# Layer 2's weights summed and parked in DRAM during layer 1, its activation moved into the first product, and its second product done with seven products

## The chip, the cores and the metric

One core of a Trainium2 chip runs the whole program. The metric is the device time of one execution in microseconds (us). The profile is one execution taken by the hardware profiler; its span, from the first to the last instruction, is a little shorter than the execution's own time.

## The reference

The program computes windowed attention (4 batches, 8 heads, 576 positions, head size 64, each position sees itself and the 63 before it), then two MLPs over the 2304 tokens of 512 features, each with 2048 hidden features:

```python
scores = np.matmul(q, k.transpose(0, 1, 3, 2)) / np.sqrt(D)
mask = (rel >= 0) & (rel < 64)
attn = softmax(np.where(mask, scores, -1e9))
x = np.matmul(attn, v)                                   # to (2304, 512)

h = x @ w_in;   x = np.maximum(0.01 * h, h) @ w_out      # layer 1, moe_*
h = x @ w_in;   g = np.maximum(h, 0) + np.log1p(np.exp(-np.abs(h)))
out = (g @ w_out).astype(np.float32)                     # layer 2, moe2_*
```

All four weight matrices arrive as 64-bit floats.

## The kernel before, in words

**Numbers.** A 64-bit weight tile (128 x 512) is narrowed to 32 bits by one instruction on ACT and two on DVE (`conv_a`, `conv_b`). Every product is made from two halves of each operand: ACT writes a rounded copy (hi, type fp32r), DVE subtracts it from the value (lo), and `three` issues three matmuls for each product: hi with hi, hi with lo, lo with hi (lines 531 to 533).

**Stages.** A head, written out item by item in the string `HEAD`, loads q, k, v and layer 1's weights, does the first attention blocks and starts layer 1; the order of its items is fixed on every engine. Layer 1 walks six chunks of 384 tokens (`c`); for each of 16 feature blocks `j` it has 12 matmuls of 384 columns (`gemm1`), the activation, the two halves (`gh`, `gl`) and, two steps later (`SKEW`), 12 matmuls into four banks (`gemm2`). The attention of a later chunk is spread over these steps (`attention_slots`); from tile 6 on, q and k are loaded in transposed 32 x 32 blocks straight from the inputs (`load_blocks`). The result of layer 1 goes to DRAM (`x2d`).

Layer 2's **first product** (`products`, lines 604 to 640) uses Winograd's form of Strassen's method: a pair `p` of feature blocks and a chunk `c` of 768 tokens make a 2 x 2 block problem, done with 7 products instead of 8. There are 8 pairs and 3 chunks, 24 steps; a step has 7 products of 6 matmuls with 384 columns each. The sums of tokens (`split_x2`) and of weights (`conv_pair`) are made on DVE by `winograd`, the results are joined by one copy on ACT and seven adds on DVE that read PSUM (line 630), and h goes to DRAM (`hd`). Each pair's weights are loaded, narrowed, summed and split right before their use, by a `ticker` that is called between the steps (`todo`, `prepare`, `later`).

Layer 2's **second product** (`second`) is a plain one: chunks of 512 tokens (`TO`), 16 feature blocks; for a block h is loaded, activated (`activate`: flag the sign on DVE, softplus on ACT, max and add on DVE), split, and multiplied for each of 4 groups of 128 tokens with three matmuls of 512 columns into a bank of its own. Two sets of four banks take turns.

**Queues.** All transfers are issued on the SP queue, in order. PSUM has 8 banks, in the tags `h`, `att` and `o`.

## Time and profile before

| | |
|---|---|
| median of 3 runs | 870.58 us (870.52 to 872.3) |
| the profiled execution | 870.51 us, span 868.7 us |
| TensorE's granted clock | 0.998 of full speed on average |
| PE, busy share of the span | 98%, 5424 matmuls |
| weight loads (PEld) | 92% |
| DVE, ACT, POOL | 62%, 47%, 6% |
| DMA queue, share of 16 engines | 42%, 103.84 MB |

How to read it: PE is the matrix engine, PEld its weight loads, DVE the vector engine, ACT the activation engine, POOL the GpSimd engine and SP the engine whose queue issues the transfers. A group names line, engine and operation, output <- input, shapes and how many; then its busy time, the mean of one, and the idle time before it with what ended that. Records of matmuls overlap, so the interval between two starts says more than a matmul's own duration. In a table by stage the number in brackets is the count of instructions.

### The profile page before, as it was taken

The numbers are of one execution on the slowest core, as the hardware profiler recorded it, in microseconds if no ns is written. First come the engines' busy times: TensorE is split into PE (matmuls) and PEld (weight loads), VectorE is DVE, ScalarE is ACT, GpSimd is POOL, SyncE is SP. The second block draws the span as 40 slices with busy tenths as digits, with TensorE's granted clock in tenths as the row PEclk, the third lists the DMA queues.
The fourth block names the chain that finished last, engine by engine and source line by source line (L and its number), as shares of the span: only waits on it lengthen the run. The fifth ranks groups of instructions, "written<-read, shape, count | busy, mean of one in ns | idle before, by whom it ended". The sixth has DMA issues, their size and how long they took to land.

```text
span 868.7 us, 14599 instructions
## 1 busy us (share of the span) xinstructions
PE 849.8 (98%) x5424; PEld 799.4 (92%) x5424; DVE 537.4 (62%) x1052; ACT 406.2 (47%) x966; POOL 48.7 (6%) x66
## 2 busy tenths in 40 slices
PE   6799999999999999999999999999999999999998
PEld 5689999999999999999999999999999888888886
DVE  5798852535334323323258599777799986766664
ACT  5887742544444334444356433222245654545443
POOL 3211000111111011100000000000000000000000
PEclk9999999999999999999999999999999999999999
DMA  9768552253233421200223245444487553434332
GB/s 206 195 196 244 169 123 36 56 96 89 32 60 75 81 51 49 59 3 13 75 97 102 83 159 191 158 158 158 163 309 260 165 155 102 142 100 142 101 103 66
DMA packets 150278, 104.76 MB, mean 121 GB/s; under 512 B 104896, under 2 KB 129472, under 8 KB 150208
## 3 DMA queue, kind: packets, MB, share of 16 engines
q1 hardware_dynamic: 150208, 103.84, 42.0%
q8 instruction: 42, 0.69, 0.3%
q14 instruction: 28, 0.23, 0.1%
HBM read 75.50 MB, written 28.31 MB: 119 GB/s over the span
## 4 chain that ended last, share of the span: by engine, by line
PE 90%; DVE 3%; DMA 3%; ACT 1%; issue 1%; SPq 1%; POOL 0%; ACTq 0%; DVEq 0%
PE f L533 8%; PE f L532 8%; PE f L531 8%; PE o L531 7%; PE ph L531 7%; PE o L532 7%; PE o L533 7%; PE ph L533 7%; PE ph L532 7%; PE p_s L533 4%; PE p_s L531 4%; PE p_s L532 4%; PE p_a L533 3%; PE p_a L531 3%; PE p_a L532 3%; DMA wraw<-in_moe_w_out_dram 2%
## 5 line engine op out<-in xcount | busy, mean ns | idle before, releaser
L563 DVE TENSOR_TENSOR gl<-g,gh 128x384 fp32r<-128x384 f32 x96 | 57.2, 596 | 174.8 <-ACT gh L557 130.9
L531 PE MATMUL o<-gh,w 128*128 128x384 f32 x384 | 130.9, 341 | 1.9 <-ACT part L577 1.5
L531 PE MATMUL ph<-xh,w 128*128 128x384 f32 x384 | 130.4, 340 | 0.0
L532 PE MATMUL o<-gl,w 128*128 128x384 f32 x384 | 128.7, 335 | 0.7 <-DVE gl L563 0.6
L533 PE MATMUL ph<-xh,w 128*128 128x384 f32 x384 | 128.4, 334 | 0.0
L532 PE MATMUL ph<-xl,w 128*128 128x384 f32 x384 | 128.3, 334 | 0.0
L533 PE MATMUL o<-gh,w 128*128 128x384 f32 x360 | 120.4, 334 | 0.0
L551 ACT ACTIVATE g<-ph 128x384 f32<-128x384 f32 x96 | 46.9, 488 | 144.9 <-PE ph L533 143.6
L531 PE MATMUL f<-w,s 128*128 128x512 f32 x234 | 91.0, 389 | 0.0
L532 PE MATMUL f<-w,s 128*128 128x512 f32 x234 | 91.0, 389 | 0.0
L533 PE MATMUL f<-w,s 128*128 128x512 f32 x234 | 91.0, 389 | 0.0
L662 ACT ACTIVATE s<-s 128x512 f32<-128x512 f32 (+1 forms) x80 | 46.8, 588 | 72.6 <-DVE s L661 72.2
L531 PEld LDWEIGHTS o<-gh,w 128*128 128x128 f32 x384 | 72.1, 188 | 4.4 <-ACT part L577 1.8
L532 PEld LDWEIGHTS o<-gl,w 128*128 128x128 f32 x384 | 72.1, 188 | 1.4 <-DVE gl L563 1.2
L664 DVE SCALAR_TENSOR_TENSOR s<-s,s 128x512 f32<-128x512 f32 (+1 forms) x80 | 50.7, 637 | 36.4 <-ACT s L662 36.0
L531 PEld LDWEIGHTS ph<-xh,w 128*128 128x128 f32 x384 | 72.1, 188 | 1.0 <-issue 0.5
L532 PEld LDWEIGHTS ph<-xl,w 128*128 128x128 f32 x384 | 72.2, 188 | 0.0
L533 PEld LDWEIGHTS ph<-xh,w 128*128 128x128 f32 x384 | 72.1, 188 | 0.0
L533 PEld LDWEIGHTS o<-gh,w 128*128 128x128 f32 x360 | 67.6, 188 | 0.0
L439 ACT ACTIVATE sm<-sm,nm 128x128 f32<-128x128 f32 x144 | 56.0, 391 | 19.6 <-DVE nm L428 19.5
L234 DVE TENSOR_TENSOR s<-s,s 128x512 fp32r<-128x512 f32 (+1 forms) x80 | 50.7, 636 | 12.7 <-ACT s L233 12.5
L233 ACT CAST s<-s 128x512 fp32r<-128x512 f32 (+1 forms) x80 | 46.0, 576 | 23.1 <-PE f L532 20.0
(169 smaller groups left out, 1643.6 us busy)
## 6 DMA issues: line engine op xcount, KB each, us to landing
wraw<-in_moe_w_out_dram SPq DMA_DIRECT2D x32, 512.0 KB, 4.8
wraw<-in_moe_w_in_dram SPq DMA_DIRECT2D x32, 512.0 KB, 4.7
s<-hd SPq DMA_DIRECT2D x64, 256.0 KB, 2.7
hd<-h_xh SPq DMA_DIRECT2D x12, 768.0 KB, 4.5
hd<-h_xl SPq DMA_DIRECT2D x12, 768.0 KB, 4.2
x2d<-x SPq DMA_DIRECT2D x24, 192.0 KB, 1.9
x_stage<-x2d SPq DMA_DIRECT2D x24, 192.0 KB, 2.6
out_dram<-s SPq DMA_DIRECT2D x18, 256.0 KB, 2.4
```

The source lines that it names most:

```text
L233: i = nc.scalar.copy(hi, a)
L234: j = nc.vector.tensor_tensor(lo, a, hi.bitcast(F32), ALU.subtract)
L439: nc.scalar.activation(sm[:, p, :], sm[:, p, :], AF.Exp, bias=nm[:, p : p + 1], accum_out=sums[:, p : p + 1],)
L531: nc.tensor.matmul(ps, wh, xh, start=start, stop=False)
L532: nc.tensor.matmul(ps, wh, xl, start=False, stop=False)
L533: nc.tensor.matmul(ps, wl, xh, start=False, stop=stop)
L551: nc.scalar.activation(g, ph, AF.Prelu, alpha=0.01)
L563: b = nc.vector.tensor_tensor(gl, g, gh.bitcast(F32), ALU.subtract)
L662: nc.scalar.activation(g, g, AF.Softplus)
L664: nc.vector.scalar_tensor_tensor(g, h, 0.0, g, ALU.max, ALU.add)
```

## The change

- Layer 2's weights are handled in layer 1's chunks 2 to 5, 32 units in all (`stash`): load, narrow, add the four sums on POOL, write to DRAM (`wd`). For `w_out` they are summed over the other index. The last six units (pairs 5 to 7 of `w_out`) are also split there. Later a pair is loaded ready-summed (`load_row`) and split (`split_pair`): the low half on DVE for `w_in`, on POOL for `w_out`; pairs 5 to 7 need no split.
- q and k from tile 6 on are first laid out in DRAM (`lay_out`, DRAM to DRAM in 128-byte pieces, partly during the head) and loaded from there in one transfer each.
- The sums of x for the first product move from DVE to POOL, and the four that are split get a place of their own (`split_sums`).
- The activation follows each step of the first product: sign flag on DVE, softplus and relu on ACT, add on POOL, and the activated value goes to `hd`.
- The second product uses seven products as well. A step is a pair of feature blocks and 512 tokens (256 in the last chunk): four sums (`sums`) and three low halves on DVE, three hi copies on ACT (`spread`), then per product 3 matmuls of 256 columns for each 256 tokens. Seven banks collect a chunk; at its end `put_out` joins them by the same copy and seven adds. The order on every engine is fixed from the second product on (`ordered`).

```diff
@@ -64,6 +64,7 @@
     CUT = 8
     TB = 32
     BY_DVE = 6
+    THIRDS = 10
     AHEAD = 4
...
     hd = [dp.tile([P, 2, NT], F32, name=f"hd{p}") for p in range(NF // 2)]
+    HD = DM // 2
+    PARTS = 2 * NP * (P // TB)
+    qd, kd = (dp.tile([P, NP, NT], F32, name=f"{nm}d") for nm in "qk")
+    SPLIT, SPAN = 5, 88
+    split_too = lambda i, p: i == 1 and p >= SPLIT
+    wd = [
+        [dp.tile([P, 8, 2, 2, P] if split_too(i, p) else [P, 8, 2, P], F32, name=f"wd{i}_{p}") for p in range(NF // 2)]
+        for i in range(2)
+    ]
 
...
+    ODD = (("v", 3, 1), ("kT", 2, 1), ("qbd", 1, 2), ("part", 1, 3))
+    EVEN = (("raw", 2, 1),) * 2 + (("v", 3, 1),) * 2 + (("sm", 3, 1),) * 2 + (("kT", 2, 1),)
+    ENDS = (("xh", 2, 3), ("xl", 2, 3), ("w_last", 1, 1))
...
+    def load_row(i, p, row, o):
+        if split_too(i, p):
+            nc.sync.dma_start(row.bitcast(F32), wd[i][p][:, o].rearrange("p a h x -> p a (h x)"))
+        else:
+            nc.sync.dma_start(row[:, 1].bitcast(F32), wd[i][p][:, o].rearrange("p h x -> p (h x)"))
...
+        for t in pair_tiles.pop((i, p)):
+            split(t[:, :, 0], t[:, :, 1], t[:, :, 1].bitcast(F32), nc.gpsimd if i == 1 else None)
+
...
+    def stash_load(u):
+        i, p, q = units[u]
+        j = slice(2 * p * P, 2 * (p + 1) * P)
+        if i == 0:
+            src = moe2_w_in[:, j].rearrange("(h q p) f -> p q h f", p=P, q=2)[:, q]
+        else:
+            src = moe2_w_out[j, q * HD : (q + 1) * HD].rearrange("(f p) x -> p f x", p=P)
+        nc.sync.dma_start(raw_of(u).rearrange("p (n x) -> p n x", n=2), src)
+
...
+        def sums_of(u):
+            t = blocks(a_of(u))
+            b = [[t[:, n], t[:, m]] for n, m in ((0, 2), (1, 3))]
+            if units[u][0] == 1:
+                b = [list(x) for x in zip(*b)]
+            winograd([t[:, 4 + n] for n in range(4)], b, units[u][0] == 0, nc.gpsimd)
...
+        at, end = {}, 0
+        light = sum(not has_low(u) for u in range(len(units)))
+        for u in range(len(units)):
+            parts = [(0, stash_load, u + 1), (0, narrow_a, a_of, u), (1, narrow_b, a_of, u), (2, sums_of, u)]
+            if has_low(u):
+                parts += [(2, high, u, 0), (3, low, u, 0), (3, high, u, 1), (4, low, u, 1)]
+            parts += [(7 if has_low(u) else 5, put, u)]
+            for n, *do in parts:
+                at.setdefault(end + n, []).append(do)
+            end = (u + 1) * SPAN // light if u + 1 <= light else end + 4
+        stash_load(0)
+        for n in range(max(at) + 1):
+            yield
+            for f, *x in at.get(n, ()):
+                if x[0] is a_of:
+                    f(a_of(x[1])[:, :DM], raw_of(x[1]))
+                elif f is not stash_load or x[0] < len(units):
+                    f(*x)
+        kept["end"] = True
 
     def key(g):
         return g if isinstance(g, int) else "%d_%d" % g
...
+    def lay_out(b, parts):
+
+
+        for n in parts:
+            src, dst = ((q, qd), (k, kd))[n % 2]
+            p, i = divmod(n // 2, P // TB)
+            h, d = divmod(i * TB, D)
+            s0 = max(BY_DVE * P - b * S, 0)
+            nc.sync.dma_start(
+                dst[i * TB : (i + 1) * TB, p, b * S + s0 : (b + 1) * S].rearrange("r (n c) -> r n c", c=TB),
+                src[b, 2 * p + h, s0:, d : d + TB].rearrange("(n r) c -> r n c", r=TB),
+            )
...
                 for n in range(7)
             ]
-        winograd([ts[:, n] for n in range(4)], b, False)
-        for d, a in zip(XB[c], (b[0][0], b[1][0], b[1][1], *(ts[:, n] for n in range(4)))):
+        winograd([ts[:, n] for n in range(4)], b, False, nc.gpsimd)
+        for d, a in zip(XB[c], (b[0][0], b[1][0], b[1][1])):
             split(d[:, 0, kk], d[:, 1, kk], a)
+
+    def split_sums(c, kk):
+        for n, d in enumerate(XB[c][3:]):
+            split(d[:, 0, kk], d[:, 1, kk], stage["t"][:, n])
 
 
     G = {}
...
+    ORDER = ((0, 0), (5, 4), (6, 5), (4, 3), (2, 1), (7, 2), (3, 6))
...
+        behind.append(
+            combine(
+                (product(*o) for o in ORDER), t("q1"), t("u2"), t("u3"), t("v"),
+                ((h[:, 0, :TH], h[:, 0, TH:]), (h[:, 1, :TH], h[:, 1, TH:])),
+            )
+        )
+        for a in range(2):
+            g = next(act_places)
+            nc.vector.tensor_scalar(g.bitcast(I32), h[:, a].bitcast(I32), -(2**31), None, ALU.bitwise_or)
+            nc.scalar.activation(g, g, AF.Softplus)
+            nc.scalar.activation(h[:, a], h[:, a], AF.Relu)
+            nc.gpsimd.tensor_tensor(g, h[:, a], g, ALU.add)
+            nc.sync.dma_start(hd[p][:, a, c * 2 * TH : (c + 1) * 2 * TH], g)
+
...
+    def sums(i):
+        m = steps2[i][2] // 2
+        h = HT["in"][i % HS][:, :2, : 2 * m]
+        st = kept["64"][1 + i % 2].bitcast(F32)
+        ts = st[:, : 4 * m].rearrange("p (n x) -> p n x", n=4)
+        ready[i] = h, ts
+        winograd([ts[:, x] for x in range(4)], [[h[:, c, r * m : (r + 1) * m] for c in range(2)] for r in range(2)], True)
+
+    def places_of(i):
+        w0, w1, *one = sets[i % SETS]
+        m = steps2[i][2] // 2
+        one = [w[:, :m] for w in one]
+        two = [w[:, 2, : 2 * m].rearrange("p (a x) -> p a x", a=2) for w in (w0, w1)]
+        four = [w[:, :2].rearrange("p a x -> p (a x)")[:, : 4 * m].rearrange("p (n x) -> p n x", n=4) for w in (w0, w1)]
+        return one, two, four, m
+
+    def spread(i):
+        one, two, four, m = places_of(i)
+        h, ts = ready.pop(i)
+        parts = (two, h[:, :, :m]), (one, h[:, 1, m:]), (four, ts)
+        first = [nc.scalar.copy(hi, a) for (hi, lo), a in parts][0].ins
+        last = [nc.vector.tensor_tensor(lo, a, hi.bitcast(F32), ALU.subtract) for (hi, lo), a in parts][-1].ins
+        behind.append((first, last))
+        A[i] = {0: [t[:, 0] for t in two], 2: [t[:, 1] for t in two], 3: one}
+        for x in range(4):
+            A[i][4 + x] = [t[:, x] for t in four]
+
+    def advance(i):
+
+        for f, n in ((sums, 3), (spread, 2), (load_h, 5)):
+            if (HS if f is load_h else 0) <= i + n < len(steps2):
+                f(i + n)
+
+    R = {}
+
...
+    def second(i):
...
+            if first:
+                R[k][x] = next_bank([P, 2, HD], f"f_{k}_{x}")
+            wh, wl = w[USED[ob]]
+            before = None
+            for u in range(nu):
+                cs = slice(u * P, (u + 1) * P)
+                gh, gl = (t[:, cs] for t in a[oa])
+                ps = R[k][x][:, u]
+                j = nc.tensor.matmul(ps, gh, wh, start=first and u == 0, stop=False, skip_group_check=True)
+                if before is not None:
+                    tc.add_manual_dep(
+                        j.ins, before.name,
+                        mybir.DependencyInfo(mybir.DependencyClass.NoSync, mybir.DependencyReason.DATA),
+                        reason="bank",
+                    )
+                nc.tensor.matmul(ps, gh, wl, start=False, stop=False, skip_group_check=True)
+                j = nc.tensor.matmul(ps, gl, wh, start=False, stop=end, skip_group_check=True)
+                before = j.ins
+            return R[k][x][:, :nu]
+
+        made = [product(x) for x in range(7)]
+        if end:
+            split_out = lambda t: t.rearrange("p u (q x) -> p u q x", q=2)
+            ends[i] = [split_out(t) for t in made], [split_out(t[:, :nu]) for t in stage["t4"]]
+
+    ends = {}
...
+    def put_out(i):
+        if i in ends:
+            k, t0, n, p = steps2[i]
+            made, temps = ends.pop(i)
+            res = [r[:, : n // (2 * P)] for r in stage["res"]]
+            halves = [r.rearrange("p u (q c x) -> p u q c x", q=2, c=2) for r in res]
+            combine(iter(made), *temps, [[r[:, :, :, c] for c in range(2)] for r in halves])
+            for r in range(2):
+                r0 = t0 + r * (n // 2)
+                nc.sync.dma_start(out[r0 : r0 + n // 2, :].rearrange("(u p) d -> p u d", p=P), res[r])
+
+    def last_places():
...
+    relay = {f"G{CUT + NF - AHEAD - 2 + n}": (lay_out, first, range(n * PARTS // 2, (n + 1) * PARTS // 2)) for n in range(2)}
+    relay |= {f"G{CUT + NF - AHEAD + n}": (lay_out, first + 1, range(n * PARTS // 4, (n + 1) * PARTS // 4)) for n in range(4)}
...
             slot += 1
             if u == 0:
...
+                later(next, keeper, None, lag=1)
+        if c == 0 and j >= NF - 4:
+            lay_out(3, range(4 * (j + 4 - NF), 4 * (j + 5 - NF)))
+        if c == 2 and 4 <= j < 12:
...
-
+    todo[1] += [(split_x, 2, 0), (split_sums, 2, 0), (load_x, 2, 1)]
+    todo[2] += [(split_x, 2, 1), (split_sums, 2, 1)]
+    for p in range(2, NPR):
+        n = last_of[p - 2] if p < NPR - 1 else 8
+        todo[n] += [(load_first, p)]
+        todo[n + 2] += [(split_pair, 0, p)]
...
+    def load_second(p):
+        if p == 0:
+            tiles = tiles_of((("at", 2, 1),) * 2, "wp1_0") + early(5)
+        elif p == 1:
+            tiles = early(7)
+        else:
+            tiles = tiles_of((ODD, ENDS, EVEN)[p - 2], f"wp1_{p}")
+        load_pair(1, p, tiles)
+
+    def temporaries():
+        stage["t4"] = [w[:, 2].rearrange("p (u x) -> p u x", u=2) for w in HT["in"]]
...
+    todo[N - 3] += [(load_second, 2), (split_pair, 1, 1)]
+    todo[N - 2] += [(advance, -1), (load_second, 3)]
+    todo[N - 1] += [(last_places,), (split_pair, 1, 2), (load_second, 4)]
     for n, (p, c) in enumerate(order):
         products(n, p, c)
...
+        next(rows)
+    late = [rows for rows in late for n in range(7)]
+    temporaries()
     for i in range(len(steps2)):
-        second(*steps2[i], active.pop(i))
-        activate_next(i + 3)
-        load_next(i + 6)
-        if i % 2:
-            later(next, last, None)
+        ordered(queues, second, i)
+        ordered(queues, advance, i)
+        if i < 2:
+            ordered(queues, split_pair, 1, 3 + i)
+        for n in range(4):
+            if late:
+                ordered(queues, next, late.pop(0))
+        ordered(queues, put_out, i)
 
 
 # ---- launch: one core; inputs and outputs as the reference has them ----
```

Where the order shows it. On PE, the start of the second product (`f` is a bank; before, the moving operand is a row of `w_out`, afterwards a row of a pair's weights `wp`, `wq`). Before:

```order
L531 MATMUL f_0_7347<-w2xh,s_7067 128x512
L532 MATMUL f_0_7347<-w2xl,s_7067 128x512
L533 MATMUL f_0_7347<-w2xh,s_7068 128x512
L531 MATMUL f_1_7348<-w2xh,s_7067 128x512
L532 MATMUL f_1_7348<-w2xl,s_7067 128x512
L533 MATMUL f_1_7348<-w2xh,s_7068 128x512
```

Now:

```order
L792 MATMUL f_0_7676<-wp_0_at_7129,a_0_7125 128x256
L799 MATMUL f_0_7676<-wp_0_at_7129,a_0_7125 128x256
L800 MATMUL f_0_7676<-wp_0_at_7129,a_1_7126 128x256
L792 MATMUL f_0_7676<-wp_0_at_7129,a_0_7125 128x256
L799 MATMUL f_0_7676<-wp_0_at_7129,a_0_7125 128x256
L800 MATMUL f_0_7676<-wp_0_at_7129,a_1_7126 128x256
L792 MATMUL f_1_7683<-wq_5_7131,a_0_7125 128x256
```

A bank now takes two groups of three, each of half the columns, with a weight load before every matmul as before.

On ACT, in the first product around the copies of the first bank of steps 8 and 9 (`q`; `h_xh` and `h_xl` take turns as h). Before:

```order
L632 COPY q_8_6115<-p_a_6119 128x384
L159 ACTIVATE cvp_10_6327<-wraw_10_0_6323 128x512
L233 CAST wp_v_6248<-cvp_9_6110 128x256
L233 CAST wp_raw_6246<-cvp_8_6109 128x512
L233 CAST wp_v_6249<-tt_6241 128x512
L159 ACTIVATE cvp_11_6328<-wraw_11_0_6325 128x512
L632 COPY q_9_6179<-p_a_6183 128x384
```

Now:

```order
L699 ACTIVATE kept_2_1589<-kept_2_1589 128x768
L700 ACTIVATE h_xl<-h_xl 128x768
L699 ACTIVATE cv<-cv 128x768
L700 ACTIVATE h_xl<-h_xl 128x768
L707 COPY q_8_6318<-p_0_6322 128x384
L236 CAST wp_4_raw_6389<-wp_4_raw_6389 128x256
L236 CAST wp_4_sm_6393<-wp_4_sm_6393 128x256
```

The four activations of step 7 (line 699 is softplus, 700 relu) stand between the splits before them and the copy of step 8's first bank.

On DVE, in the second product at the end of the first chunk (`in` is h as loaded or a temporary, `kept` the sums, `a` the halves, `res` the output). Now:

```order
L760 TENSOR_TENSOR a_1_7126<-in_7120,a_0_7125 128x512
L760 TENSOR_TENSOR a_gl<-in_7120,a_gh 128x256
L760 TENSOR_TENSOR a_1_7126<-kept_2_1589,a_0_7125 128x1024
L706 TENSOR_TENSOR in_7120<-f_1_7683,in_7119 128x512
L706 TENSOR_TENSOR in_7121<-f_2_7690,in_7120 128x512
L706 TENSOR_TENSOR in_7365<-f_3_7697,in_7120 128x512
L706 TENSOR_TENSOR res_xl<-f_3_7697,in_7121 128x4x128
L706 TENSOR_TENSOR res_xh<-f_4_7704,in_7119 128x4x128
L706 TENSOR_TENSOR res_xh<-f_5_7711,in_7365 128x4x128
L706 TENSOR_TENSOR res_xl<-f_6_7718,in_7121 128x4x128
L255 TENSOR_TENSOR kept_2_1589<-in_7365 128x256 x2
```

The seven adds that empty a chunk's banks come after the low halves for two steps ahead and before the next sums; before, a chunk was emptied by four copies on ACT and four on DVE between the activations.

## Rows read from the trace of the kernel before

**Rows 1.** Busy time by stage; columns: stretch, us, busy us and instructions by engine, clock, DMA.

```profile
0.00:91.40 91.40, 76.77 (x612) 69.96 (x612) 72.68 (x142) 70.08 (x198) 17.87 (x32) 0.98 0.80 208
91.40:493.80 402.40, 402.16 (x2940) 392.65 (x2941) 173.17 (x340) 183.72 (x486) 30.88 (x34) 1.00 0.28 68
493.80:668.60 174.80, 174.80 (x1010) 174.80 (x1009) 149.82 (x298) 53.35 (x100) 0.00 (x0) 1.00 0.57 195
668.60:864.70 196.10, 196.10 (x866) 162.04 (x864) 141.14 (x272) 98.69 (x183) 0.00 (x0) 1.00 0.41 121
```

**Rows 2.** What PE waited for, 91.4 to 868 us: total, times, longest in us.

```profile
PE o L531 <- ACT part L577: 1.5, 1, 1.5
PE ps L703 <- ACT at L467: 0.2, 1, 0.2
```

**Rows 3.** Timeline of PE, first product: start us, us, instruction.

```profile
499.83 0.33 PE L532 MATMUL p_s<-xb,wp_sm 128*128 128x384 f32 x1
...
501.91 0.33 PE L532 MATMUL p_a<-xb,wp_raw 128*128 128x384 f32 x1
```

**Rows 4.** Timeline of PE, second product.

```profile
759.82 0.39 PE L531 MATMUL f<-w2xh,s 128*128 128x512 f32 x1
...
761.86 0.39 PE L531 MATMUL f<-w2xh,s 128*128 128x512 f32 x1
```

**Rows 5.** Instruction groups, second product: count, busy us, mean ns, idle before.

```profile
L531 PE MATMUL f<-w,s 128*128 128x512 f32 x234 | 91.0, 389 | 0.0
L531 PE MATMUL f<-w2xh,s 128*128 128x512 f32 x54 | 21.0, 389 | 0.0
```

**Rows 6.** 128-column matmuls of the head, and weight loads.

```profile
12.97 1.17 PE L413 MATMUL ps<-kT,qbd 128*128 128x128 f32 x9
...
L413 PE MATMUL ps<-kT,qbd 128*128 128x128 f32 x96 | 13.3, 294 | 0.0
L413 PEld LDWEIGHTS ps<-kT,qbd 128*128 128x128 f32 x96 | 12.8, 212 | 0.1
L531 PEld LDWEIGHTS f<-w,s 128*128 128x128 f32 x234 | 43.9, 188 | 9.1
```

**Rows 7.** Instruction groups on DVE.

```profile
L234 DVE TENSOR_TENSOR s<-s,s 128x512 fp32r<-128x512 f32 x64 | 43.9, 689 | 7.5 <-ACT s L233 7.5
L661 DVE TENSOR_SCALAR s<-s 128x512 int32<-128x512 int32 x64 | 26.9, 425 | 1.6 <-DMA s<-hd 0.2
L630 DVE TENSOR_TENSOR v<-p_s,u 128x384 f32<-128x384 f32 x24 | 13.4, 559 | 5.5 <-PE p_s L533 5.4
L234 DVE TENSOR_TENSOR wp_qbd<-cvp,wp_qbd 128x256 fp32r<-128x256 f32 x4 | 1.7, 420 | 0.0
```

**Rows 8.** Instruction groups on ACT and POOL.

```profile
L662 ACT ACTIVATE s<-s 128x512 f32<-128x512 f32 x64 | 40.1, 631 | 66.0 <-DVE s L661 65.7
L632 ACT COPY q<-p_a 128x384 f32<-128x384 f32 x24 | 11.4, 474 | 65.5 <-PE p_a L533 59.7 <-DVE xb L234 5.9
L452 POOL TENSOR_TENSOR sm<-sm,sums 128x512 f32<-128x512 f32 x36 | 38.7, 1075 | 147.3 <-DVE sums L448 103.1 <-PE o L532 23.3 <-ACT w L221 11.3
```

**Rows 9.** Instruction groups of a weight's conversion.

```profile
L159 ACT ACTIVATE cvp<-wraw 128x512 f32<-128x512 f32 x28 | 18.7, 674 | 13.0 <-DMA wraw<-in_moe_w_out_dram 9.2 <-DVE h_xl L630 3.7 <-DMA wraw<-in_moe_w_in_dram 0.2
L176 DVE SCALAR_TENSOR_TENSOR cvp<-wraw,cvp 128x512 uint16<-128x512 uint32 x32 | 23.7, 751 | 0.2
```

**Rows 10.** Timeline of the end, PE and DVE.

```profile
864.32 0.39 PE L533 MATMUL f<-w,s 128*128 128x512 f32 x1
...
865.14 0.42 DVE L680 COPY s<-f 128x256 f32<-128x256 f32 x1 [0.26 <-ACT s L679]
```

**Rows 11.** Timelines of DVE and POOL in layer 1.

```profile
255.41 1.09 DVE L563 TENSOR_TENSOR gl<-g,gh 128x384 fp32r<-128x384 f32 x1 [0.54 <-ACT gh L557]
...
255.04 1.04 POOL L452 TENSOR_TENSOR sm<-sm,sums 128x512 f32<-128x512 f32 x1 [0.52 <-DVE sums L448]
...
306.77 0.56 DVE L563 TENSOR_TENSOR gl<-g,gh 128x384 fp32r<-128x384 f32 x1
```

412 lines of the change are left out of this document (200 added, 212 removed).

## The prediction

> **What bounds the kernel now.** The first view to read is the table of busy time by stage [rows 1]. The span falls into a head up to 91.4 us, layer 1 up to 493.8, layer 2's first product up to 668.6 and its second product up to 864.7. The granted clock is 0.98 in the head and 1.00 afterwards, the upper of TensorE's two levels, 2.4 GHz. After the head PE is busy for 402.16 of 402.40 us, then for all of 174.80 and all of 196.10. Busy time alone proves little, since the records of matmuls overlap; so the second view is what PE waited for [rows 2]: 1.7 us in two places in layer 1, nothing in layer 2. Third, the starts: in the first product 12 intervals of a 384-column matmul lie between 499.83 and 501.91 us, 173.3 ns each [rows 3]; in the second, 9 intervals of a 512-column matmul between 759.82 and 761.86, 226.7 ns each [rows 4]. The first product has 24 steps of 42 matmuls: 1008 x 173.3 ns = 174.7 us. The second has three lines of 234 + 54 matmuls [rows 5]: 864 x 226.7 ns = 195.9 us. Both are the stage's length within 0.2 us. So layer 2 is a string of matmul starts without a hole. It gets shorter only through fewer columns, and longer only when something that feeds PE comes too late. DVE is the busiest feeder: 149.82 of 174.80 us in the first product. POOL does nothing in layer 2 [rows 1].
>
> **Second product by seven.** The new loop has 7 products per pair of feature blocks, for each 3 matmuls per unit of 256 tokens: 42 in a step of 512 tokens, 21 in the last chunk's. Four chunks of 8 pairs and one short one give 32 x 42 + 8 x 21 = 1512 matmuls of 256 columns, in place of 864 of 512: an eighth fewer columns. No row shows this kind of matmul with 256 columns. The line through the two nearest rows falls by 53.4 ns per 128 columns (226.7 - 173.3), so 256 columns would follow every 119.9 ns, and the stage would take 1512 x 0.120 = 181.4 us. From above it is bounded by the 384-column matmul, 173.3 ns: 262.0 us. From below by 128-column matmuls of the head: nine in 1.17 us, of which the last takes some 0.294, so (1.17 - 0.294) / 8 = 110 ns [rows 6]: 166.3 us. What could lift it off the line is the weight load that goes with every matmul, since it has to be over within one interval. Loads of the second product last 188 ns in the records, those of the head's 128-column matmuls 212 ns, and those pass every 110 ns all the same [rows 6]; so a load should fit under 120 ns. I take the line: 195.9 - 181.4 = **14.5 us less**. Break-even is 195.9 / 1512 = 129.6 ns.
>
> The Trainium skill's page TensorE: Matmul & The Clock Gate, Back-to-back issue gap, gives columns / 2.4 + 2.5 ns, which is 109 ns for 256 columns and would make the stage 165 us. For 512 columns it gives 216 ns where the row shows 226.7, so here the rows decide.
>
> **What feeds the second product.** A full step lasts 42 x 0.120 = 5.04 us on PE. On DVE it has four sums of 256 columns at 0.42 us [rows 7] and three low halves of 512, 256 and 1024 columns at 0.69, 0.42 and (an estimate: the first two rows' slope carried on) 1.23 us: 4.0 us. At the end of a chunk seven adds out of PSUM come on top, 512 columns wide; at 0.56 for 384 [rows 7] that is 0.69 each by the same slope, 4.9 us. Eight steps: 37 of 40.3 us. These adds stand in DVE's queue behind the halves for two steps ahead, which PE needs only 5 us later, and a chunk's eighth bank lets the next one begin before they are through. Cost nothing; if DVE were 10% dearer it would set the pace.
>
> **Activation inside the first product.** A step is 42 x 173.3 = 7.28 us. It keeps ACT's copy and DVE's seven adds (7 x 0.56 = 3.9), and gets two flag instructions on DVE over 768 columns (at most 1.5 x 0.425 = 0.64 each [rows 7]), four activations on ACT (at most 1.5 x 0.631 = 0.95 [rows 8]) and two adds on POOL (at most 1.5 x 1.075 = 1.6 [rows 8]). With about 0.8 us of weight splits DVE comes to 6.0, ACT to some 5, POOL to 3.2: each fits. The wait that it adds: a step's activations stand in ACT's queue ahead of the next step's copy of its first bank. That copy, 0.47 us [rows 8], ends at most 0.56 + 0.64 + 4 x 0.95 + 0.47 = 5.5 us after the step's end; PE wants the bank eight products later, 8.3 us after it. Covered with 2.8 us to spare, so nothing. The 150 us of DVE lose the weight conversions and the sums of x, which is the room for it.
>
> **Weights summed in layer 1.** 32 units, each one ACT instruction of 0.67 us and two on DVE of at most 0.75 [rows 9], four POOL sums; the last six also split. ACT gets 22 us more and DVE at most 48, in 402.40 us where they are busy for 183.72 and 173.17 [rows 1]. PE uses a step's halves two steps (8 us) later, so a queue that is a few us late costs nothing. Traffic: 16.8 MB read, some 20 MB written, 6.3 MB more for the relay of q and k, 43 MB or 107 GB/s on top of 68 [rows 1]; the first product moves 195 GB/s without a wait of PE. The SP queue carries writes that wait for POOL ahead of loads of q, k and v; the next tile's loads have some 20 us. Nothing; 0 to +5 at the bounds.
>
> **Head and tail.** Eleven relay transfers are issued between the last weight loads of layer 1, when PE has work in hand: 0 to +1. At the end the last matmul starts at 864.32, the last copy at 865.14, and the output lands at 868.7 [rows 10]. Afterwards adds of 256 columns (about 0.42) trail a product of 0.36 us, and DVE is an instruction further behind: +0.5.
>
> **Sum.** The profiled execution took 870.51 us, 1.8 more than its span, and 0.07 less than the median of 870.58. 870.51 - 14.5 + 0.5 = **856.5 us**.
>
> **Rivals.** *The weight load shows.* On top of 384 / 2.4 = 160 ns of columns the row has 13 ns more [rows 3]. If that stretch followed not the columns but a load of 110 ns, the interval would be 123 to 126 ns, the stage 186 to 190.5 us, the time 861 to 866. For it: load and columns are about equally long here for the first time. Against it: the head's short matmuls have no such stretch.
>
> *A shorter interval*, the 110 ns of the 128-column rows: 166.3 us, time 841. Against it speaks the fixed 13 ns in both stages of layer 2. The Trainium skill's 109 ns (TensorE: Matmul & The Clock Gate, Back-to-back issue gap) would lead to the same place.
>
> *Slower: DVE blocked by POOL in the first product.* In layer 1 a DVE instruction with both operands in SBUF began at 255.41, while a POOL multiply ran from 255.04 to 256.08; it took 1.09 us, where the same line took 0.56 at 306.77, and ended 0.4 after POOL's [rows 11]. POOL, now idle there, would work 3.2 us of each step, plus the sums of x and the splits of five pairs near the hand-over. If three quarters of a step's 3.2 us fall on flags and splits, DVE needs 6.0 + 2.4 = 8.4 us against 7.28, and 24 steps cost 27 us: 883. It decides once the blocked time passes 1.3 us a step and eats the gain at 1.9. Against it: POOL starts when ACT is through, so while DVE does adds out of PSUM, and no row shows those blocked. The Trainium skill's page SBUF — State Buffer, Who interferes with whom, calls this an exclusive lock held for the whole instruction, and its rule spares adds that read PSUM. The trace agrees for the blocked instruction.
>
> *The eighth goes, but the time doesn't.* The weights of pairs 5 to 7 get their places only when the first product ends, and the writes of its last steps share the queue; or layer 1 stalls on a queue. A dozen us lost gives 866 to 871.
>
> **Chances.** The forecast 0.65 (its own range 854 to 861), the load 0.13, the shorter interval 0.04, DVE blocked 0.11, the gain lost 0.07. A measurement tells about 0.2% from no change. The first three are faster: 0.82; the lost gain is the same: 0.07; the blocked DVE slower: 0.11. The range 853 to 871 leaves out the shorter interval and the slower case, 0.15, and a little of the rest.
>
> **What would show it.** Starts of 256-column matmuls 120 ns apart, the second product's stage near 181 us, the first still 174.7 with no wait of PE in the list, layer 1 over at 494. Flags of 0.6 us on DVE; 1.5 or more there, and PE waiting for adds, would mean the block. 125 ns between starts would mean the load. It is wrong if PE waits over 5 us in layer 2, or if the first product's stage grows.

## The result and the profile after

The changed kernel takes 883.59 us (median of 4 runs, 879.79 to 886.33), the kernel before, beside it, 870.55 us (869.98 to 872.3). The ratio is 1.0143, with a 95% interval of 1.0096 to 1.019: 1.4% slower, clear of no change, outside the range, and close to the 883 that the prediction had given to its slower rival. The profiled execution took 881.52 us with a span of 879.7, against 870.51 and 868.7 before. (In the text VectorE is DVE of the rows, ScalarE is ACT, and a place is a stretch of SBUF, the core's on-chip memory, that the program uses in turns.)

The first view is again the table by stage, now of the changed kernel (stretch, length, busy us and instructions of PE, PEld, DVE, ACT and POOL, granted clock, DMA share, GB/s). It answers to [rows 1].

```profile
0.00:91.40 91.40, 79.09 (x626) 72.59 (x627) 75.00 (x147) 72.22 (x201) 18.18 (x32) 0.98 0.83 211
91.40:492.70 401.30, 399.81 (x2928) 389.75 (x2928) 212.08 (x382) 203.65 (x525) 110.39 (x178) 1.00 0.65 172
492.70:691.00 198.30, 182.88 (x1011) 178.09 (x1009) 171.26 (x276) 107.05 (x178) 108.35 (x63) 0.97 0.48 160
691.00:875.40 184.40, 182.09 (x1512) 181.65 (x1512) 155.86 (x298) 79.26 (x134) 20.48 (x14) 1.00 0.47 151
```

Layer 1 ends 1.2 us earlier than before (the first product starts at 492.72 instead of 493.94), although it now holds the stash of weights. The first product, which took 174.80 us, takes 198.30; the second, which took 196.10, takes 184.40. In starts of matmuls: -1.2 before the first product, +22.5 in it (197.0 us from its first start to its last, 174.5 before), +1.1 between the two, -11.3 in the second (184.4 against 195.7), nothing at the tail. That is +11.1 us, and the spans differ by 11.0.

The second view is the list of PE's waits after the head, which held 1.7 us before [rows 2].

```profile
PE p L593 <- DVE u L706: 7.6, 7, 2.5
PE p L593 <- DVE h_xl L706: 3.9, 1, 3.9
PE f L792 <- DVE h_xl L706: 2.3, 1, 2.3
PE p L593 <- ACT q L707: 1.7, 2, 1.1
PE p L593 <- DVE h_xh L706: 1.3, 1, 1.3
```

The banks of the first product (p) come free too late, because VectorE's adds out of them are late. Third, the starts of the second product's matmuls, which answer to [rows 4]: nine intervals lie between these two rows.

```profile
759.75 0.28 PE L800 MATMUL f<-wq,a 128*128 128x256 f32 x1
...
760.83 0.28 PE L800 MATMUL f<-wq,a 128*128 128x256 f32 x1
```

That is 120.0 ns for 256 columns, the value that the line through the two older rows gave. So the eighth was gained, and lost again, twice over, in the stage before. Why VectorE is late there is seen in two timelines of the same four microseconds, VectorE first and then POOL (start us, us, instruction; "x2" joins two in a row).

```profile
509.25 1.74 DVE L237 TENSOR_TENSOR xb<-x_stage,xb 128x384 fp32r<-128x384 f32 x1
510.91 0.55 DVE L706 TENSOR_TENSOR h_xl<-p,u 128x384 f32<-128x384 f32 x1
511.38 1.74 DVE L698 TENSOR_SCALAR kept<-h_xl 128x768 int32<-128x768 int32 x1
```

```profile
508.40 4.30 POOL L701 TENSOR_TENSOR cv<-h_xh,cv 128x768 f32<-128x768 f32 x2
```

While POOL does its two adds (508.40 to 512.70), a low half of 384 columns takes VectorE 1.74 us, where it took 0.55 before, and ends 0.42 us after the first of the two adds (508.40 to 510.57). The flag takes 1.74, where 0.55 is its time with POOL at rest, and ends 0.42 us after the second. The add that reads a PSUM bank stands between them and takes its usual 0.55. A hole of PE follows where several such instructions meet in a row (VectorE, POOL, then PE):

```profile
568.21 2.61 DVE L237 TENSOR_TENSOR wp_xh<-wp_xh 128x768 fp32r<-128x768 f32 x1
570.74 2.56 DVE L237 TENSOR_TENSOR wp_xl<-wp_xl 128x768 fp32r<-128x768 f32 x1
573.23 0.55 DVE L706 TENSOR_TENSOR u<-p,q 128x384 f32<-128x384 f32 x1
```

```profile
568.04 1.96 POOL L701 TENSOR_TENSOR cv<-h_xh,cv 128x768 f32<-128x768 f32 x1 [3.49 <-ACT h_xh L700]
569.96 2.53 POOL L701 TENSOR_TENSOR kept<-h_xh,kept 128x768 f32<-128x768 f32 x1
```

```profile
570.96 0.34 PE L595 MATMUL p<-xb,wp_part 128*128 128x384 f32 x1
573.83 0.44 PE L593 MATMUL p<-xb,wp_part 128*128 128x384 f32 x1 [2.53 <-DVE u L706]
```

POOL is held in turn: its second add takes 2.53 us, where 1.92 is the mean of its kind, and VectorE's `wp_xh` runs into it until 570.82.

For each run below two numbers are taken from its trace. **Lost time** is what VectorE's instructions of the first product took beyond the time of the same form with POOL at rest (0.41 us for 256 columns, 0.55 for 384, 0.68 for 512, 0.95 for 768, 1.22 for 1024, 0.55 for a flag), counted where it is over 0.15 us. **Holes** are the time from the start of that stage's first matmul to the end of its last, less 1008 x 173.3 ns. The changed kernel has 40.1 us lost in 35 instructions and 22.6 us of holes. All 161 adds out of PSUM in its records took 0.55 us, 84 of them with POOL at work. Of VectorE's instructions that leave PSUM alone, 38 began while POOL was computing. 35 of these lost time, and they are all that did; each ended within its own usual time after the end of the POOL instruction beside which it had begun.

### The profile page after: what moved, and what is told of

The parts are those of the page before. It is cut to its first block, busy times and chain, and to the rows that moved or that the text cites. A ratio compares the mean times of both kernels' runs of the same rounds, so it can differ in the third digit from the quotient of the medians.

```text
span 879.7 us, 16530 instructions
## 1 busy us (share of the span) xinstructions
PE 844.1 (96%) x6072; PEld 822.1 (93%) x6072; DVE 615.3 (70%) x1104; ACT 462.2 (53%) x1037; POOL 257.4 (29%) x287
## 5 line engine op out<-in xcount | busy, mean ns | idle before, releaser
L625 DVE TENSOR_TENSOR gl<-g,gh 128x384 fp32r<-128x384 f32 x96 | 59.9, 624 | 130.6 <-ACT gh L619 108.0
L792 PE MATMUL f<-wq,a 128*128 128x256 f32 x252 | 71.4, 283 | 0.0
L799 PE MATMUL f<-wq,a 128*128 128x256 f32 x252 | 71.3, 283 | 0.0
L800 PE MATMUL f<-wq,a 128*128 128x256 f32 x252 | 71.3, 283 | 0.0
L510 POOL TENSOR_TENSOR sm<-sm,sums 128x512 f32<-128x512 f32 x36 | 38.6, 1072 | 87.7 <-DVE sums L506 54.3
L759 ACT CAST a<-in 128x512 fp32r<-128x512 f32 (+1 forms) x40 | 23.0, 576 | 56.7 <-issue 46.8
L760 DVE TENSOR_TENSOR a<-kept,a 128x1024 fp32r<-128x1024 f32 (+1 forms) x40 | 47.9, 1197 | 6.7 <-ACT a L759 6.7
L619 ACT CAST gh<-g 128x384 fp32r<-128x384 f32 x96 | 49.3, 514 | 2.4
```

The lines of the kernel that those rows point to most:

```text
L510: nc.gpsimd.tensor_tensor(sm, sm, sums.unsqueeze(2).to_broadcast([P, NP, P]), ALU.mult)
L619: a = nc.scalar.copy(gh, g)
L625: b = nc.vector.tensor_tensor(gl, g, gh.bitcast(F32), ALU.subtract)
L760: last = [nc.vector.tensor_tensor(lo, a, hi.bitcast(F32), ALU.subtract) for (hi, lo), a in parts][-1].ins
L792: j = nc.tensor.matmul(ps, gh, wh, start=first and u == 0, stop=False, skip_group_check=True)
L799: nc.tensor.matmul(ps, gh, wl, start=False, stop=False, skip_group_check=True)
```

## The experiments

Three theories stood. *Lock*: VectorE's instructions whose operands all lie in SBUF stand still while POOL works there. *ScalarE's queue*: softplus and relu stand ahead of the next step's bank copy. *SP's queue*, added later: the store waits for POOL's add, and loads of weights stand behind it. The edits are in `products` unless said otherwise. The kernel before, measured beside each group of runs, had medians of 870.6 to 872.3 us, so 1 to 2 us between runs of different groups say little.

### Without POOL's add

```diff
-            nc.gpsimd.tensor_tensor(g, h[:, a], g, ALU.add)
```

> Edit: in the first product POOL's add of the relu and the softplus is left out (the softplus alone is stored, so this part of the activation is not computed); flags, softplus, relu, transfers and every order stay. Lock theory (VectorE's instructions whose operands all lie in SBUF stand still while POOL runs: 40.9 us of VectorE time lost in the first product, and TensorE's 23.5 us of holes come from there): POOL falls from 108 to about 25 us in that stage, the lost VectorE time to under 12 us, the holes to under 6 us, the time to 862 to 867 us. Queue theory (ScalarE's softplus and relu stand ahead of the next step's bank copy, and VectorE waits 20.3 us for that copy): nothing in that queue changes, the holes stay at 18 us or more, the time at 878 us or more.

856.73 us, ratio 0.9834 (0.9804 to 0.9865). Lost time 9.6 us, holes 0.2. Its two stages of layer 2:

```profile
493.40:668.10 174.70, 174.70 (x1010) 174.70 (x1009) 144.01 (x279) 107.88 (x180) 23.73 (x19) 1.00 0.54 183
668.10:849.60 181.50, 181.50 (x1513) 181.36 (x1511) 151.29 (x296) 78.44 (x133) 12.07 (x10) 1.00 0.46 152
```

PE is busy throughout both again, 174.7 and 181.5 us long. The split that took 2.61 us takes 0.95:

```profile
L237 DVE TENSOR_TENSOR wp_xh<-wp_xh 128x768 fp32r<-128x768 f32 x1 | 0.9, 950 | 0.0
```

So the whole loss comes through this one instruction per half step; the forecast for everything else in the change holds.

### Without the relu

```diff
-            nc.scalar.activation(h[:, a], h[:, a], AF.Relu)
```

> Edit: in the first product ScalarE's two relu per step are left out (POOL adds the softplus to the plain value, so this part of the activation is not computed); POOL's add stays. Queue theory: the chain copy, seven adds, flag, softplus and relu is 7.15 us long where no wait lengthens it, against 7.28 us of TensorE per step; without the relu it is about 5.7, VectorE's 20.3 us of waits for the copy fall under 5 and the time to 860 to 867 us. Lock theory: POOL still runs 108 us in that stage and VectorE still loses about 40 us; with 171 us of work in 174.7 us most of the holes stay: 872 us or more.

887.72 us, ratio 1.0187 (1.0165 to 1.021). VectorE's waits for the copy fall from 20.3 to 1.5 us, as the queue theory said, and the holes stay: 24.4 us, with 40.4 lost. The order on ScalarE does not make the loss by itself. But the edit changes something else too: VectorE now waits for casts of weights instead (11.2 us for those of one group of tiles), while SP stands 130 us at stores that wait for POOL.

### Softplus and relu a step later

The flags stay; the rest is collected in a list and issued after the next step's copy.

```diff
+        with tc.issue_after(behind[-1][0]):
+            activate(stage.pop("due", ()))
+        if n < len(order) - 3:
+            stage["due"] = due
...
```

> Edit: nothing is left out; softplus and relu of a step are issued behind the next step's bank copy, in all steps but the last three, which stay as in the changed kernel. VectorE's waits for the copy fall from 20 to under 3 us, its standstills beside POOL stay near 40 us. Standstills alone: between the changed kernel's 883.6 and 876; with both needed for the loss it would be 866 us or less.

875.1 us, ratio 1.0043 (1.0026 to 1.006); lost 44.4, holes 13.8. In the last seven steps only three places take turns, and a late activation reads a place that a newer flag has overwritten: that part of the activation is changed there. A first form, late in every step, gave 876.78 us with 41.8 lost and 10.6 of holes; 860 to 867 us had been expected of it if the queue makes the loss, 872 or more if the lock does. The standstills are as long as ever, but fewer of them reach PE: the order decides how many.

### POOL's other work on VectorE

```diff
-        winograd([ts[:, n] for n in range(4)], b, False, nc.gpsimd)
+        winograd([ts[:, n] for n in range(4)], b, False)
...
-            split(t[:, :, 0], t[:, :, 1], t[:, :, 1].bitcast(F32), nc.gpsimd if i == 1 else None)
+            split(t[:, :, 0], t[:, :, 1], t[:, :, 1].bitcast(F32))
```

> Edit: nothing is left out; POOL's other work of the first product and the start of the second (block sums of the input, low halves of layer 2's second weights, 24.5 us on POOL in that stage) goes to VectorE, the activation's add stays on POOL. Lock theory: VectorE takes about 11 us of work more and loses about 9 us less to POOL: within 5 us of the changed kernel's 883.6. Queue theory: the same, no change. If the late holes (after 640 us, where POOL's low halves lie and the clock falls to half) come from those low halves, the time falls by 5 to 8 us.

877.12 us, ratio 1.0064 (1.0042 to 1.0086); lost 28.2, holes 16.7. Less on POOL helps even where VectorE has to do it. Both theories had expected no more than 5 us; the 6.5 that came lie in the 5 to 8 which the expectation gave to the low halves late in the stage.

### The add aside

```diff
-            nc.gpsimd.tensor_tensor(g, h[:, a], g, ALU.add)
+            nc.gpsimd.tensor_tensor(h[:, a], h[:, a], h[:, a], ALU.add)
```

> Edit: POOL's add stays in place and length, but adds the relu to itself in its own place, and nothing waits for it but the next use of that place; the softplus alone is stored (this part of the activation is not computed). It parts POOL's presence from POOL's place in the chain to the store. If VectorE's standstills beside POOL make the loss: the first product loses what the changed kernel loses, 878 to 888 us. If the loss came because stores, places and loads waited for POOL's result: 857 to 864 us, as without the add.

868.03 us, ratio 0.9952 (0.9937 to 0.9968): neither of the two. Lost 29.6, holes 9.6. The instruction is not the twin that it was meant to be: with one place instead of two it takes 1.57 us in place of 1.92. So POOL's presence alone costs some 11 us against the run without it. How much of the other 15 us is the shorter instruction and how much the store that no longer waits for POOL, this run by itself does not tell; but SP still stood 101 us at those stores, now waiting for ScalarE, against 123 us in the changed kernel.

### The add by an accumulating transfer

```diff
-            nc.gpsimd.tensor_tensor(g, h[:, a], g, ALU.add)
+            nc.gpsimd.dma_start(out=g, in_=h[:, a], accum_op=ALU.add)
```

> Edit: nothing is left out; the add of relu and softplus is made by an accumulating transfer from POOL's queue, SBUF to SBUF, ahead of the store, instead of by POOL itself. If POOL's own instruction on SBUF is what stops VectorE, the loss goes as without the add: 857 to 864 us, VectorE's lost time under 16 us. If the extra 0.39 MB per half step, or the work of POOL in issuing it, gets in the way (transfers already take 48% of the queues in that stage), 865 us or more, with waits for places.

903.0 us, ratio 1.0354 (1.0326 to 1.0382). The lost time is gone, 8.8 us, and the holes are 38.5. SP's stores now wait for the accumulating transfers, and its loads of weights wait behind them (what SP waited for, from 493 to 705 us):

```profile
SPq L702 <- DMA kept<-h_xh: 44.6, 10, 13.1
SPq L702 <- DMA cv<-h_xh: 27.6, 9, 9.8
SPq L702 <- DMA kept<-h_xl: 22.7, 8, 5.3
SPq L702 <- DMA cv<-h_xl: 17.0, 5, 6.4
```

ScalarE stands 17.7 us at the casts of one group of weights, 55.5 us at all of them, with the bank copy behind it. This is mostly SP's queue at work, without the lock; VectorE also waited some 20 us for places.

The same add made in DRAM, behind the store of the relu:

> Edit: nothing is left out; the relu is stored first and the softplus is then added onto it in DRAM by an accumulating transfer from POOL's queue. Same reasoning: 857 to 864 us if only POOL's instruction on SBUF costs; two transfers in a row must land before the loads of the second product, so the last step of the first product may make the second product wait some us.

902.65 us, ratio 1.0356 (1.0324 to 1.0387); lost 8.8, holes 33.4. Here the transfers from POOL took 7.4 us to land, and the flags waited 28 us for their places.

### The store from POOL's queue

```diff
-            nc.sync.dma_start(hd[p][:, a, c * 2 * TH : (c + 1) * 2 * TH], g)
+            nc.gpsimd.dma_start(hd[p][:, a, c * 2 * TH : (c + 1) * 2 * TH], g)
```

> Edit: nothing is left out; the store behind POOL's add is issued from POOL's queue instead of SP's, so that SP, whose next orders are the loads of weights, no longer stands at that store until POOL is done. Third theory (SP's queue: the store holds up weight loads, ScalarE stands at the casts of those weights, and the bank copy behind them is late): 865 to 872 us. Standstills of VectorE alone: they stay at 40 us, and the time stays above 878 us.

897.53 us, ratio 1.0299 (1.0269 to 1.0329): worse than the changed kernel. SP no longer stands at the store, ScalarE waits only 2.0 us for weights, and the holes are 37.0 all the same: they don't need SP's queue. Lost time rises to 51.7 us. VectorE's longest wait in the stage is not one for POOL's work, though the profile names POOL there. VectorE, then POOL, then the time from that store's issue to its landing:

```profile
645.50 0.42 DVE L255 TENSOR_TENSOR kept<-in 128x256 f32<-128x256 f32 x1 [3.94 <-POOL cv L701]
```

```profile
640.06 0.56 POOL L702 DMA_DIRECT2D hd<-kept  x1
DMA to landing us min/median/max: 5.4/5.4/5.4
```

The block sum writes the place `kept`, from which that store was still going out. It lands at 645.42, and the sum begins at 645.50. An issue alone did not stop VectorE either: 25 of its instructions on SBUF met nothing of POOL's but an issue, and none took over 0.02 us longer. What raised the lost time is in part this: 8 of the 32 instructions that lost time began ahead of POOL's add, in the issue before it, and 5 stood through more than one POOL instruction. Neither happened in the changed kernel. Why an issue between POOL's adds does that is open.

### The add at loading

Softplus and relu are both stored, the relu in `hr`, a second array like `hd`; in `load_h` an accumulating load adds them.

```diff
+            nc.sync.dma_start(hr[p][:, a, c * 2 * TH : (c + 1) * 2 * TH], h[:, a])
...
+            nc.gpsimd.dma_start(out=HT["in"][i % HS][:, :2, :n], in_=hr[p][:, :, t0 : t0 + n], accum_op=ALU.add)
```

> Edit: nothing is left out; POOL's add is gone from the first product, softplus and relu are both stored, and the second product's load of the softplus is followed by an accumulating load of the relu from POOL's queue (POOL has nothing else there). If POOL's instruction on SBUF beside VectorE is the cause, the first product runs without holes as in the run without the add: 856 to 862 us in all. If the accumulating loads come late, the second product waits for its block sums: 865 us or more.

951.39 us, ratio 1.0919 (1.089 to 1.0948). The first product runs nearly without holes (4.8 us, 8.6 lost), as the lock theory has it; the second takes 272.7 us. Its waits, on VectorE and on POOL:

```profile
DVE kept L256 <- DMA in<-hr: 114.6, 31, 15.5
```

```profile
POOL in L739 <- issue: 118.9, 23, 9.1
POOL in L739 <- DMA in<-hd: 50.7, 6, 14.9
```

POOL is late in issuing, for most of the time without anything that the profile names. VectorE is not what holds it: it worked on SBUF in 44.1 of those 118.9 us. The landing times show what does. All 23 issues came 0.3 us after the accumulating load before had landed, so these loads went one at a time, 6.1 us each in the median. Why they did is open; in the two runs with accumulating transfers in the first product these overlapped. By the Trainium skill's page SBUF — State Buffer, Who interferes with whom, a transfer issued by POOL can starve beside VectorE. This trace does not show that.

### Half of each add

```diff
-            nc.gpsimd.tensor_tensor(g, h[:, a], g, ALU.add)
+            nc.gpsimd.tensor_tensor(g[:, :TH], h[:, a, :TH], g[:, :TH], ALU.add)
```

> Edit: POOL adds only the first half of each place's columns (the other half of the activation lacks its relu). Dose: POOL runs some 45 us less in that stage. Standstill theory: VectorE's lost time falls from 40 to about 22 us and the loss of 27 us (883.6 against 856.7 without the add) to a half or less: 862 to 870 us. If it is POOL's being in the chain at all, not its length, 876 us or more.

858.89 us, ratio 0.9859 (0.9831 to 0.9887); lost 14.0, holes 0.2. A half of the dose leaves not a half of the loss but nearly nothing: the loss is not proportional to POOL's work. Two things help here, and this run doesn't part them: VectorE has 30.7 us of idle time in the run without the add (174.70 less 144.01) that can take some lost time, and half an add is also a shorter instruction.

### Late, and stored from POOL's queue

Softplus and relu a step later, in the first sixteen steps, and the store from POOL's queue, together.

> Edit: nothing is left out; softplus and relu are issued behind the next step's bank copy in the first sixteen steps, and the store goes from POOL's queue. Both together take away VectorE's waits for the copy and SP's stand at the store, and leave POOL's 108 us as they are. If these orders only make a given standstill dear: 863 to 870 us with VectorE's lost time still near 40 us. If the standstills alone set the loss: 872 us or more.

894.18 us, ratio 1.0275 (1.0246 to 1.0303); lost 66.0, holes 35.8. Stores from POOL's queue cost more than the order gives.

### The same work in shorter instructions

```diff
-            nc.gpsimd.tensor_tensor(g, h[:, a], g, ALU.add)
+            for b in range(2):
+                s = slice(b * 2 * TH // 2, (b + 1) * 2 * TH // 2)
+                nc.gpsimd.tensor_tensor(g[:, s], h[:, a, s], g[:, s], ALU.add)
```

Two pieces:

> Edit: nothing is left out; each add of 768 columns on POOL is two of 384 in a row, so POOL's whole time grows a little (about 2 x 1.0 us in place of 1.92) and each instruction is half as long. If VectorE stands only until the POOL instruction in hand ends and then has its turn: lost time 40 to about 25 us or less, 862 to 873 us. If it stands until POOL has no more work: lost time 40 us or more, 880 us or more.

Four pieces:

> Edit: nothing is left out; each add on POOL is four of 192 columns. If VectorE has its turn between instructions: lost time under 20 us, 858 to 868 us; POOL's own time grows by its fixed part and may become late instead. If VectorE stands until POOL has no more work: 880 us or more.

Two give 873.63 us, ratio 1.0031 (1.0017 to 1.0045), with 26.7 us lost and 11.4 of holes; four give 871.1, ratio 1.0005 (0.9988 to 1.0022), with 19.4 lost and 7.6 of holes. From the changed kernel to two and to four pieces POOL works longer, 109.8, 125.4 and 145.6 us in the stage, and VectorE loses less. Two pieces lost 1.7 us more than the 25 expected, and the times are 0.6 and 3 us above their ranges. In these runs the second product waits too: from first start to last it takes 187.0 and 189.0 us, 181.3 without the add. One group of POOL's adds in each, of the changed kernel, of two pieces and of four:

```profile
L701 POOL TENSOR_TENSOR cv<-h_xl,cv 128x768 f32<-128x768 f32 x11 | 21.5, 1966 | 22.0 <-ACT h_xl L700 22.0
```

```profile
L703 POOL TENSOR_TENSOR cv<-h_xl,cv 128x384 f32<-128x384 f32 x26 | 28.4, 1121 | 18.0 <-ACT h_xl L700 13.9 <-DVE cv L698 3.2 <-DVE kept L698 0.9
```

```profile
L703 POOL TENSOR_TENSOR cv<-h_xl,cv 128x192 f32<-128x192 f32 x52 | 35.0, 707 | 10.7 <-ACT h_xl L700 9.5 <-issue 1.2
```

So it is the length of the single instruction (1.97, 1.12, 0.71 us) that decides how much VectorE loses, not POOL's time in all: VectorE gets its turn between two. Of its instructions that lost time, all 48 with two pieces and 41 of 43 with four ended within their own usual time after the POOL instruction beside which they had begun. Two pieces and the late order:

> Edit: nothing is left out; two adds of 384 as in the run before, and softplus and relu behind the next step's bank copy in the first sixteen steps. If both the standstills and the order on ScalarE cost something: 3 to 8 us under the run with two adds alone. If the order costs nothing once the standstills are short: within 2 us of it.

870.35 us, ratio 0.9996 (0.998 to 1.0012); lost 32.3, holes 8.6. The order is worth about 3 us here.

### Looking for a version below both

Four pieces, and the low halves on POOL (`split_pair`) cut into rows of 256 columns:

```diff
...
+                nc.scalar.copy(t[:, :, 0], t[:, :, 1].bitcast(F32))
+                for n in range(t.shape[1]):
+                    lo = t[:, n, 1]
+                    nc.gpsimd.tensor_tensor(lo, lo.bitcast(F32), t[:, n, 0].bitcast(F32), ALU.subtract)
...
```

> Edit: nothing is left out; as the run with four adds, and POOL's low halves of layer 2's weights are written one row of 256 columns at a time instead of up to 768. If the late holes come from those long instructions: 2 to 6 us under the run with four adds (871.1), 865 to 869 us. If they come from the sheer amount of work of VectorE there: within 1.5 us of 871.

The same with the late order, and four pieces with POOL's other work on VectorE:

> Edit: nothing is left out; the run with all of POOL's work cut, and softplus and relu behind the next step's bank copy in the first sixteen steps. If VectorE's 19 us of waits for the copy still matter: 1 to 4 us under the run without it. If not: the same within 1.5 us.

> Edit: nothing is left out; four adds on POOL, and POOL's other work (block sums of the input, low halves) on VectorE. VectorE takes about 11 us more of work and loses some 8 us less: 863 to 870 us if its room there (30 us idle with four adds) takes it; 871 us or more if the work falls into the crowded end of the stage.

874.03 us, ratio 1.003 (1.0013 to 1.0046); 873.8, ratio 1.0026 (1.0011 to 1.004); 871.53, ratio 0.9992 (0.9972 to 1.0011). The first missed both of its ranges; the others came out as their expectations had it for no gain. The holes of the first product do shrink (6.4, 5.4 and 7.2 us, with 17.7, 21.7 and 13.2 lost), but the second product takes 192.0, 191.9 and 191.5 us from first start to last. In the first two runs PE waits early in it, mainly for low halves from POOL (these rows are the first run's); in the third, where VectorE makes them, it waits mainly for adds out of PSUM (3.4 us for `u`):

```profile
PE f L807 <- POOL wp_raw L217: 2.3, 1, 2.3
PE f L800 <- DVE h_xl L714: 1.3, 1, 1.3
PE f L807 <- POOL wp_sm L217: 1.1, 1, 1.1
```

No version with the full activation came out below the kernel before; the best are equal to it within the noise. Versions without POOL in the activation (ScalarE making the magnitude and VectorE adding, or one softplus of the plain value) were not run.

## Why the prediction was wrong, point by point

- **Second product by seven: right.** 120.0 ns and 181.5 us, against 119.9 and 181.4. The weight load did not show, and the interval was not shorter. In the changed kernel itself 3 us are lost in this stage, most of them at its start (one hole of 2.4 us); the run without the add does not have them.
- **Its feeders, the stash of weights, head and tail: right.** No wait of PE in the second product beyond its start; layer 1 ends 1.2 us earlier; the stretch from the last matmul to the end is 4.4 us as before.
- **"Activation inside the first product ... Covered with 2.8 us to spare, so nothing": the step that failed.** It took each duration from a row in which POOL was at rest, and priced POOL's adds only by POOL's own time (3.2 us a step; two of 1.94 are 3.9). What they cost is VectorE's. It lost 40.1 us in the stage, 1.67 a step, where 6.0 of 7.28 us were thought to be in use; 31.8 of the 40.1 fell on instructions that began beside these adds, the rest on such as began beside POOL's block sums and low halves. Without the add 9.6 us are lost, and the whole forecast holds: 856.73 us against 856.5.
- **The argument against the slower rival failed with it.** "POOL starts when ACT is through, so while DVE does adds out of PSUM" is only in part true: adds out of PSUM filled 30% of the time of POOL's adds, and 24 of VectorE's instructions were held up beside those adds. Between a step's adds VectorE also has halves of weights and x, and from 640 us on the block sums and halves of the second product. By kind the loss is about 16 us on halves in the first product (L237), 11 on block sums (L255), 7 on the second product's halves (L760), and only 7 on the flags. Adds out of PSUM were spared without exception (0.55 us in all, 84 of 161 beside POOL). The rule in the Trainium skill's page SBUF — State Buffer, Who interferes with whom, has it so, and the trace agrees.
- **The rival's mechanism was right, its price half luck.** It put the blocked time at 2.4 us a step and all of the excess on PE: 27 us. It was 1.67 a step, of which 0.94 reached PE. It let the loss begin at 1.3 us a step, which is VectorE's idle time without the add (30.7 us over 24 steps = 1.28). PE lost time well before that: at 19.4 us lost in all (0.8 a step, four pieces) there were 7.6 us of holes, and at 13.2 (four pieces, POOL's other work on VectorE) 7.2, though at 14.0 (half adds) none. So no single value of lost time parts runs with holes from runs without.
- **Why spare time could not be used** is partly the order on ScalarE, which the same step had judged step by step only. Copy, seven adds, flag, two softplus, two relu and the next copy form a ring. By the prediction's own bounds it takes 0.47 + 3.9 + 0.64 + 3.8 = 8.8 us, more than the 7.28 of a step, so "2.8 us to spare" could not hold step after step at these bounds. At the measured durations it just fits. On ScalarE, from one copy to the next (the 7.15 us between them hold no standstill in the ring):

```profile
562.19 0.46 ACT L707 COPY q<-p 128x384 f32<-128x384 f32 x1
...
566.38 0.85 ACT L699 ACTIVATE cv<-cv 128x768 f32<-128x768 f32 x1 [1.04 <-DVE cv L698]
567.14 0.83 ACT L700 ACTIVATE h_xh<-h_xh 128x768 f32<-128x768 f32 x1
567.87 0.83 ACT L699 ACTIVATE kept<-kept 128x768 f32<-128x768 f32 x1
568.60 0.83 ACT L700 ACTIVATE h_xh<-h_xh 128x768 f32<-128x768 f32 x1
569.34 0.46 ACT L707 COPY q<-p 128x384 f32<-128x384 f32 x1
```

  A step of PE has 7.28 us, so a standstill in the ring has next to nothing to be made up from. Taking the ring apart saved 3 us (two pieces) to 8.5 (whole adds). That it does not make the loss alone is shown by the run without the add, where the same ring stands, VectorE waits 20.7 us for the copy, and no hole is left.
- **SP's stand at the store** is there with the add and without it. What SP waited for in the first product (us in all, times, longest), in the changed kernel and then in the run without the add:

```profile
SPq L702 <- POOL kept L701: 68.5, 22, 8.1
SPq L702 <- POOL cv L701: 54.3, 20, 8.0
```

```profile
SPq L701 <- ACT kept L699: 47.6, 22, 6.7
SPq L701 <- ACT cv L699: 37.6, 20, 6.7
```

  By the third theory the stand makes weights late for ScalarE. ScalarE waited for them 8.4 us in the changed kernel, 10.6 without the add and 15.6 with half adds, and the last two have no holes. So late weights don't tell the kernel with holes from those without. The accumulating transfers show that they can matter where the wait is longer (55.5 us, 38.5 of holes).
- **What stays open:** which part of a given lost time reaches PE, since the order on ScalarE, the room that VectorE has just then and the start of the second product all have a share in it; and why stores from POOL's queue raise the lost time.

Some 5 us of the 22.6 are not waits but slow matmuls behind them. Two stretches of the changed kernel with long holes have a lower granted clock (columns as in the table by stage):

```profile
620.00:640.00 20.00, 20.00 (x117) 19.87 (x116) 15.52 (x30) 10.30 (x16) 10.20 (x8) 1.00 0.54 184
640.00:660.00 20.00, 16.97 (x88) 16.33 (x87) 19.63 (x30) 10.33 (x17) 10.35 (x7) 0.91 0.51 174
660.00:680.00 20.00, 15.05 (x76) 14.15 (x76) 20.00 (x28) 11.16 (x18) 12.69 (x7) 0.89 0.58 187
```

After PE had stood 2.0 us at 642 the clock was granted at half for 3.4 us (1.2 of 2.4 GHz), and in a stand of 3.9 us from 673 on for 6.8 us. The 2.5 us at 571 left the clock at full, so the length of one stand does not settle it. The matmuls behind the stand at 642:

```profile
645.14 0.52 PE L593 MATMUL p<-xb,wp_xl 128*128 128x384 f32 x1
645.46 0.52 PE L594 MATMUL p<-xb,wp_xl 128*128 128x384 f32 x1
```

The interval is 320 ns there, 147 more than 173.3. 42 intervals between 0.2 and 0.35 us, these and the restarts, cost 5.4 us in all.

## What to carry to other kernels

Before work is given to an idle POOL, look at what VectorE does beside it: price each POOL instruction on SBUF by its length for every VectorE instruction that may meet it with all its operands in SBUF. Set the sum against VectorE's idle time, and don't count on all of it: here, with some 30 us idle, 13 to 19 us lost could already cost PE 7. Where the work must stay there, cut it into short instructions: VectorE gets its turn between them, and here that was worth 10 to 12.5 us although POOL worked longer. And judge a queue by the ring that it closes over a whole step, not by one step's deadline.

## What the runs showed that was not expected

- Intervals of back-to-back matmuls lie on one line: 120.0 ns for 256 columns, 173.3 for 384, 226.7 for 512, which is columns / 2.4 GHz plus 13.3 ns each time. The Trainium skill's page TensorE: Matmul & The Clock Gate, Back-to-back issue gap, has 2.5 ns in that place, for a matmul by itself; for the stream of this kernel the rows decide.
- Transfers issued from POOL's queue were no way out. With the plain stores there, VectorE's lost time rose from 40.1 to 51.7 us. The accumulating ones landed 5.2 to 7.4 us after their issue in the first product, where SP's stores of the same size took 2.6 in the changed kernel; in the second product none was issued before the one ahead of it had landed.
- The loss does not go with POOL's time: with POOL at 75.6 us in the stage (half adds) there is no hole, at 109.8 us there are 22.6 us of holes, and at 145.6 us in short pieces 7.6.
